# Layer norm feeding a float32 transform on one core: tokens centered beside the root, high parts rounded with the reciprocal

## The chip, the cores and the metric

The kernel runs on one core of one Trainium2 chip. The metric is the device time of one execution in microseconds (us), the median of several runs. TensorE (PE in the profile) multiplies, VectorE (DVE), ScalarE (ACT) and GpSimd (POOL) prepare its operands, SyncE (SP) and GpSimd issue the transfers.

## The reference

`x` has 2048 tokens of 640 values. It is normalised, then transformed by DFT matrices along both axes (the real part is kept) and, beside that, passed through a gated MLP; both results are added to `x`.

```python
xn = _layernorm(x, axis=-1)                       # (x - mean) / sqrt(var + 1e-5)

# FNet part
a = einsum("bsd,ed->bse", xn, dft_hid_re)
b = einsum("bsd,ed->bse", xn, dft_hid_im)
y = einsum("ts,bse->bte", dft_seq_re, a) - einsum("ts,bse->bte", dft_seq_im, b)

# gated part, D = 640, F = 1728
gate = einsum("bsd,df->bsf", xn, W_gate)
up   = einsum("bsd,df->bsf", xn, W_up)
gate = gate * (gate > 0)
z = einsum("bsf,fd->bsd", gate * up, W_down)

return x + y + z
```

All of it is float32.

## The kernel before

Every float32 operand of a product is split in two: a high part, the value rounded by ScalarE to the type that TensorE takes (`F32R`), and a low part, the value minus the high part, by VectorE or GpSimd. A product is then three: high times high, high times low, low times high (`mm3`, L127, and for the first streams `first_products`, L492, and `next_products`, L464). TensorE therefore always waits for two other engines, and the kernel orders their work by hand: `pin` (L237) keeps instructions in program order on an engine, and the lists of work in `drive` (L701) say what is loaded, prepared and multiplied when.

The work has three stages: the DFT along the tokens, gate and up projections, and the last projections. The change is in the first 71 us of the first stage, where the tokens are normalised while the transform already runs. Tokens come in eight groups g = 0 to 7 of 256 tokens: 128 partitions with `SG` = 2 tokens j each. Columns `K14` are the first 384 of the 640, `K2` the other 256. For groups 0 to 3 only `K14` is split in high and low here and `K2` is kept as float32 by a copy (`keep_a21`, L233, a transfer on the GpSimd queue); groups 4 to 7 split all 640 columns.

Each group is multiplied by two blocks of the DFT matrix, c = 0 and c = 1 (1024 columns of 128 rows, 512 KB); a group is 36 products of 512 columns, 18 for each block. In the order of TensorE:

- group 0 (`first_products`, L500 in the profile): for token j = 0 and then j = 1, high parts of the tokens times the high half block c = 0, their low parts, the same for c = 1, then the low half blocks
- groups 1 to 7, c = 0 (`next_products`, L471): 18 products, first with the high parts of token 0 (times high and low block), then of token 1, last the low parts of both
- groups 1 to 7, c = 1 (`product`, L130 to L132)

The steps of a normalisation:

- `ln_stats` (L201): two bn_stats and a bn_aggr a token on VectorE: mean and variance
- `ln_root` (L207): on ScalarE the root of variance + eps, variance + eps itself (`ve`) and the negated mean; on VectorE the reciprocal `r0` of the root and one refinement step in three small instructions, which gives the corrected multiplier `r`
- then, in `next_group` (L245), `nmr` = -mean times r on VectorE; the high part by one ScalarE activation with scale r and bias nmr; on VectorE the normalised tokens (L265) and the low part, normalised minus high (L267)
- last on VectorE the low part of block c = 1 (L125)

The low part of the next group's block c = 0 is GpSimd's (L252, two instructions for the two tokens). A tiny GpSimd instruction ahead of it (`behind_vector`, L240) reads what VectorE writes last before, so that GpSimd starts only then. In `first_group` (L279) the two tokens are handled one after the other, the first with centered tokens (`ln_center`, `ln_scale`), the second in the way of `next_group`; the low half blocks are GpSimd's but for c = 1, j = 0, which is VectorE's (L311, L285 in the profile).

The first loads are issued by SyncE in this order (`first_stream.load`, L531): tokens j = 0, half block c = 0 of j = 0, tokens j = 1, half block c = 1 of j = 0, and the two half blocks of j = 1.

The products of groups 0 to 3 and 4 to 7 add up in the same PSUM banks. After group 3 ScalarE copies the sums so far out (`finish`, L579); the products of group 4 into a bank wait for its copy.

Of the kernel before, what the change touches and what calls it, by code (L numbers as in the profile page):

```python
# [12 lines left out]
P = 128  # L13
# [45 lines left out]
def fnet_reglu_kernel(  # L59
# [147 lines left out]
    def ln_root(g, mv, js, between=()):  # L207

        mean, v, ve, sd, r0, t = (mv[:, js, i] for i in range(6))
        nm, r = (stat[:, i, g, js] for i in range(2))  # L210
        yield nc.scalar.activation(sd, v, AF.Sqrt, bias=eps_t)
        yield nc.scalar.activation(ve, v, AF.Identity, bias=eps_t)  # L212
        yield nc.scalar.activation(nm, mean, AF.Copy, scale=-1.0)
        yield nc.vector.reciprocal(r0, sd)
        yield from between
        yield nc.vector.scalar_tensor_tensor(t, r0, -0.5, ve, op0=OP.mult, op1=OP.mult)
        yield nc.vector.tensor_tensor(t, t, r0, op=OP.mult)
        yield nc.vector.scalar_tensor_tensor(r, t, 1.5, r0, op0=OP.add, op1=OP.mult)

    def ln_center(g, xs, mv, j, cs, engine):  # L220
        xc = xs[:, j, cs]
        if engine is nc.vector:
            yield nc.vector.tensor_scalar(xc, xc, mv[:, j, 0:1], None, op0=OP.subtract)
        else:
            yield nc.scalar.activation(xc, xc, AF.Identity, bias=stat[:, 0, g, j : j + 1])

    def ln_scale(g, xs, j, cs):
        xc, r = xs[:, j, cs], stat[:, 1, g, j : j + 1]
        h, l = (tokens(g)[:, j * XS + o : j * XS + o + D][:, cs] for o in (0, D))
        yield nc.scalar.activation(h, xc, AF.Copy, scale=r)  # L230
        yield nc.vector.scalar_tensor_tensor(l, xc, r, h.bitcast(F32), op0=OP.mult, op1=OP.subtract)
# [13 lines left out]
    def next_group(g, b, raw, before):  # L245

        xs, bs, mv = ln_tiles(g)
        js = slice(0, SG)
        cs = K14 if g < NH else slice(0, D)
        nm, r = (stat[:, i, g, js] for i in range(2))  # L250
        nmr = mv[:, js, 6]
# [8 lines left out]
        pin([nc.vector.tensor_tensor(nmr, nm, r, op=OP.mult)])  # L260
        pin(nc.scalar.activation(xn_block(g, cs, 0)[:, j], xs[:, j, cs], AF.Identity,  # L261
                                 bias=mv[:, j, 6:7], scale=stat[:, 1, g, j : j + 1]) for j in range(SG))
        if before is None:
            low(nc.vector, slice(0, W2))
        pin(nc.vector.tensor_scalar(xs[:, j], xs[:, j], mv[:, j, 0:1], stat[:, 1, g, j : j + 1],  # L265
                                    op0=OP.subtract, op1=OP.mult) for j in range(SG))
        late["ln"] = pin([nc.vector.tensor_tensor(xn_block(g, cs, 1), xs[:, :, cs], xn_block(g, cs, 0).bitcast(F32),  # L267
                                                  op=OP.subtract)])[0].ins
        if g < NH:
            keep_a21(g)  # L270
        if g == NG - 1:
            nc.sync.dma_start(rows.rearrange("m (g p j) -> p m g j", p=P, j=SG), stat)
        if g == 2:
            st = stage()[:, :CH].rearrange("p (j d) -> p j d", j=SG)
            for j in range(SG):
                pin([nc.scalar.activation(st[:, j], ln_place(0)[:, j, K2], AF.Copy, scale=stat[:, 1, 0, j : j + 1])])
            keep_a21(0, st)

    def first_group(b):  # L279


        xs, bs, mv = ln_tiles(0)
        part = lambda c, j: b[c][1][:, j * CH : (j + 1) * CH]
        high = lambda c, j: pin([nc.scalar.activation(b[c][0][:, 0, j], part(c, j), AF.Copy)])
        low = lambda c, j, engine: pin([engine.tensor_tensor(b[c][0][:, 1, j], part(c, j), b[c][0][:, 0, j].bitcast(F32),  # L285
                                                             op=OP.subtract)])
        d0, d14, rest = slice(0, P), slice(P, 3 * P), slice(P, D)
        places = lambda j: [tokens(0)[:, j * XS + o : j * XS + o + D] for o in (0, D)]
# [5 lines left out]
        h0, h14 = ln_scale(0, xs, 0, d0), ln_scale(0, xs, 0, d14)  # L294
        pin([next(h0)])
        pin(ln_center(0, xs, mv, 0, rest, nc.vector))
        pin([next(h14)])
# [6 lines left out]
        nm, r, nmr = stat[:, 0, 0, j1], stat[:, 1, 0, j1], mv[:, 1, 6:7]  # L304
        h, l = places(1)
        pin(ln_stats(0, xs, bs, mv, j1))
        pin(ln_root(0, mv, j1))
        high(0, 1)
        pin([nc.vector.tensor_tensor(nmr, nm, r, op=OP.mult)])
        pin(nc.scalar.activation(h[:, cs], xs[:, 1, cs], AF.Identity, bias=nmr, scale=r) for cs in (d0, d14))  # L310
# [8 lines left out]
        pin(ln_center(0, xs, mv, 1, K2, nc.scalar))  # L319
# [203 lines left out]
    def first_stream(c, name, g):  # L523
# [7 lines left out]
        def load():  # L531
            if n == 0 and c == 0:
# [15 lines left out]
        def prepare():  # L548
# [4 lines left out]
            if (n > 0 or c > 1) and "b" not in t:  # L553
                t["b"] = b = parts()
                with ExitStack() as order:
                    if c == 1:
                        order.enter_context(tc.issue_after(late["ln"]))
                    i = split(flat(b, 0), flat(b, 1), t["s"])
# [7 lines left out]
        def run():  # L566
# [3 lines left out]
            if n > 0 and c == 0:  # L570
                next_products(n, t["b"])
                return
# [5 lines left out]

        def finish():  # L579
            if g == NH - 1:  # L580
                s = (sums_a, sums_b)[c % 2]()
                for i, key in enumerate((("e1", 0), ("e1", 1), "v1")):
                    copy(s[:, i], E[c, key])
# [702 lines left out]
```

## Time and profile before

| | us |
|---|---|
| median of 3 runs | 1033.83 (1033.81 to 1034.27) |
| the profiled execution | 1033.63 |
| its span, first to last instruction | 1031.9 |
| TensorE busy | 1024.6 (99%) |
| VectorE busy | 801.1 (78%) |
| ScalarE busy | 430.1 (42%) |
| GpSimd busy | 117.3 (11%) |

The granted TensorE clock was 1.000 over the run. Rows of the timeline begin with the start in us from the start of the span and the duration in us; then come engine, line of the kernel, operation, output and input by the program's names, and how many instructions were merged (x18). What stands in brackets is the idle time before and what ended it. In rows by form the three numbers are the shortest, median and longest instruction in ns.

### The profile page before, as it was taken

How to read it: one execution, taken by the hardware profiler on the slowest of the kernel's cores; microseconds unless marked ns; L12 is line 12 of the kernel's file. 1: busy time of each engine (PE TensorE's matmuls, PEld its weight loads, DVE VectorE, ACT ScalarE, POOL GpSimd, SP SyncE). 2: the span in 40 equal slices, each digit the busy share in tenths (PEclk: the TensorE clock that was granted, in tenths of full speed). 3: DMA queues.
4: the chain of work that ended last, by engine and by line, in shares of the span. 5: the costliest groups of instructions: out<-in, count | busy, mean ns of one | idle time of the engine just before them, and what ended most of it. 6: DMA issues, size and time to landing. Idle time of an engine off the chain costs nothing.

```text
span 1031.9 us, 12494 instructions
## 1 busy us (share of the span) xinstructions
PE 1024.6 (99%) x4528; PEld 844.7 (82%) x4528; DVE 801.1 (78%) x1074; ACT 430.1 (42%) x544; POOL 117.3 (11%) x184
## 2 busy tenths in 40 slices
PE   9999999999999999999999999999999999999998
PEld 7878888888888888888888888888778888888886
DVE  7777887998989576788878988886497667886764
ACT  6654453343443333433335443443365423552521
POOL 3431001012110002321110001000000000000000
PEclk9999999999999999999999999999999999999999
DMA  8878734867968885763364665662798637986543
GB/s 307 304 266 301 261 132 167 328 234 242 372 236 314 319 308 169 253 217 133 145 246 148 221 234 215 228 256 102 240 341 294 195 126 227 377 304 214 159 154 122
DMA packets 101469, 242.73 MB, mean 235 GB/s; under 512 B 11552, under 2 KB 50976, under 8 KB 98848
## 3 DMA queue, kind: packets, MB, share of 16 engines
q1 hardware_dynamic: 83664, 171.68, 48.6%
q0 software_dynamic: 17744, 70.26, 18.3%
q8 instruction: 35, 0.57, 0.2%
q14 instruction: 26, 0.21, 0.1%
HBM read 182.12 MB, written 58.74 MB: 233 GB/s over the span
## 4 chain that ended last, share of the span: by engine, by line
PE 96%; DVE 2%; DMA 1%; ACT 1%; issue 0%; SPq 0%; DVEq 0%; ACTq 0%
PE ps L132 31%; PE ps L131 31%; PE ps L130 31%; PE ps L471 3%; PE ps L1183 1%; DMA rw<-hd 1%; DVE bs L204 0%; DMA r<-in_x 0%; ACT xs_late L261 0%; ACT xs_early L261 0%; ACT mv L212 0%; DVE mv L205 0%; DVE r L265 0%; DVE cb L125 0%; SPq L1190 0%
## 5 line engine op out<-in xcount | busy, mean ns | idle before, releaser
L130 PE MATMUL ps<-cb,wt 128*128 128x512 f32 x390 | 151.9, 390 | 0.6 <-ACT wt L124 0.6
L132 PE MATMUL ps<-cb,wt 128*128 128x512 f32 x390 | 151.9, 390 | 0.4 <-DVE wt L125 0.4
L131 PE MATMUL ps<-cb,wt 128*128 128x512 f32 x390 | 151.8, 389 | 0.0
L125 DVE TENSOR_TENSOR cb<-rw,cb 128x1024 fp32r<-128x1024 f32 x83 | 93.9, 1132 | 70.8 <-ACT cb L124 70.1
L124 ACT ACTIVATE cb<-rw 128x1024 fp32r<-128x1024 f32 x83 | 82.0, 988 | 151.7 <-PE ps L132 127.3
L124 ACT ACTIVATE cb<-raw 128x1024 fp32r<-128x1024 f32 x71 | 75.3, 1061 | 123.0 <-PE ps L132 106.3
L125 DVE TENSOR_TENSOR cb<-raw,cb 128x1024 fp32r<-128x1024 f32 x71 | 86.7, 1222 | 35.7 <-ACT cb L124 35.5
L130 PE MATMUL ps<-xs_early,gw 128*128 128x512 f32 x260 | 101.2, 389 | 0.0
L131 PE MATMUL ps<-xs_early,gw 128*128 128x512 f32 x260 | 101.2, 389 | 0.0
L132 PE MATMUL ps<-xs_early,gw 128*128 128x512 f32 x260 | 101.1, 389 | 0.0
L130 PE MATMUL ps<-cb,xs_late 128*128 128x512 f32 x232 | 90.2, 389 | 0.0
L131 PE MATMUL ps<-cb,xs_late 128*128 128x512 f32 x232 | 90.2, 389 | 0.0
L132 PE MATMUL ps<-cb,xs_late 128*128 128x512 f32 x232 | 90.2, 389 | 0.0
L121 ACT ACTIVATE gw<-z 128x1024 fp32r<-128x1024 f32 (+1 forms) x52 | 57.6, 1109 | 76.4 <-DVE z L793 76.4
L130 PE MATMUL ps<-cb,xs_early 128*128 128x512 f32 x226 | 87.9, 389 | 0.0
L131 PE MATMUL ps<-cb,xs_early 128*128 128x512 f32 x226 | 87.9, 389 | 0.0
L132 PE MATMUL ps<-cb,xs_early 128*128 128x512 f32 x226 | 87.9, 389 | 0.0
L130 PEld LDWEIGHTS ps<-cb,wt 128*128 128x128 f32 x390 | 73.2, 188 | 16.2 <-ACT wt L124 1.0
L132 PEld LDWEIGHTS ps<-cb,wt 128*128 128x128 f32 x390 | 73.2, 188 | 15.8 <-DVE wt L125 0.7
L131 PEld LDWEIGHTS ps<-cb,wt 128*128 128x128 f32 x390 | 73.2, 188 | 15.6 <-DVE cb L125 0.3
L121 ACT ACTIVATE u<-ps 128x512 f32<-128x512 f32 x52 | 31.1, 597 | 94.4 <-PE ps L132 94.4
L803 DVE TENSOR_TENSOR gw<-z,gw 128x1024 fp32r<-128x1024 f32 (+1 forms) x52 | 64.6, 1282 | 3.8 <-ACT gw L121 3.8
(197 smaller groups left out, 1981.0 us busy)
## 6 DMA issues: line engine op xcount, KB each, us to landing
raw<-in_dft SPq DMA_DIRECT2D x94, 512.0 KB, 5.5
wt<-wparts SPq DMA_DIRECT2D x66, 256.0 KB, 3.2
z<-in_wgu SPq DMA_DIRECT2D x26, 640.0 KB, 3.9
hd<-ob POOLq DMA_DIRECT2D x26, 512.0 KB, 3.7
rw<-hd SPq DMA_DIRECT2D x24, 512.0 KB, 6.6
wparts<-pw POOLq DMA_DIRECT2D x11, 1024.0 KB, 4.1
tk<-in_dft SPq DMA_DIRECT2D x16, 512.0 KB, 6.7
set<-r POOLq DMA_DIRECT2D x16, 512.0 KB, 3.3
```

The lines of the kernel that those rows point to most:

```text
L121: return nc.scalar.activation(o, i, AF.Copy)
L124: nc.scalar.activation(hi, src, AF.Copy)
L125: return nc.vector.tensor_tensor(lo, src, hi.bitcast(F32), op=OP.subtract)
L130: nc.tensor.matmul(ps, wh, mh, start=first, stop=False, skip_group_check=more)
L131: nc.tensor.matmul(ps, wh, ml, start=False, stop=False, skip_group_check=more)
L132: nc.tensor.matmul(ps, wl, mh, start=False, stop=last, skip_group_check=more)
L471: start["pe"] = pin([nc.tensor.matmul(E[0, key], xn_part(n * SG + j, d)[v == 1], b[:, int(v == 2), j], start=False, stop=n % NH == NH - 1 ...
L803: tt(self.w[:, 1, cs], self.z[:, cs], self.w[:, 0, cs].bitcast(F32), op=OP.subtract)
L1183: nc.tensor.matmul(B[key], wr[:, v, es], hr[:, cs], start=False, stop=v == 1, skip_group_check=not new)
```

## The change

- After the root, VectorE centers the tokens in place (`ln_center`, now on VectorE always), in `next_group` one token ahead of the reciprocal and one behind it.
- The high part is the centered token times the reciprocal `r0` (`ln_high`), without the refinement. The low part is centered token times the corrected `r`, minus the high part, in one scalar_tensor_tensor a token (`ln_low`). `nmr` is gone.
- `ve` is computed on VectorE, within `ln_refine`; the negated mean is an activation of its own (`ln_mean`).
- For groups 1 to 3 the columns `K2` are normalised by an instruction of their own for each token.
- In `first_group` both tokens go the same way; the low half block c = 1, j = 0 stands ahead of the second token's statistics on VectorE. In group 1 the low part of block c = 0 is two instructions.
- SyncE issues the half block c = 1, j = 0 ahead of the tokens j = 1.
- The copies of the sums of block c = 0 after group 3 are pinned on ScalarE, right behind group 4's high parts (`keep_first`).

```diff
-    def ln_root(g, mv, js, between=()):
+    def ln_first(g, mv, js):
         mean, v, ve, sd, r0, t = (mv[:, js, i] for i in range(6))
-        nm, r = (stat[:, i, g, js] for i in range(2))
-        yield nc.scalar.activation(sd, v, AF.Sqrt, bias=eps_t)
-        yield nc.scalar.activation(ve, v, AF.Identity, bias=eps_t)
-        yield nc.scalar.activation(nm, mean, AF.Copy, scale=-1.0)
-        yield nc.vector.reciprocal(r0, sd)
-        yield from between
+        return nc.scalar.activation(sd, v, AF.Sqrt, bias=eps_t), lambda: nc.vector.reciprocal(r0, sd)
+
+    def ln_mean(g, mv, js):
+        return nc.scalar.activation(stat[:, 0, g, js], mv[:, js, 0], AF.Copy, scale=-1.0)
+
+    def ln_refine(g, mv, js):
+        mean, v, ve, sd, r0, t = (mv[:, js, i] for i in range(6))
+        yield nc.vector.tensor_scalar(ve, v, EPS, None, op0=OP.add)
         yield nc.vector.scalar_tensor_tensor(t, r0, -0.5, ve, op0=OP.mult, op1=OP.mult)
         yield nc.vector.tensor_tensor(t, t, r0, op=OP.mult)
-        yield nc.vector.scalar_tensor_tensor(r, t, 1.5, r0, op0=OP.add, op1=OP.mult)
+        yield nc.vector.scalar_tensor_tensor(stat[:, 1, g, js], t, 1.5, r0, op0=OP.add, op1=OP.mult)
...
+    def ln_center(xs, mv, j, cs):
         xc = xs[:, j, cs]
...
+        return nc.vector.tensor_scalar(xc, xc, mv[:, j, 0:1], None, op0=OP.subtract)
...
+    def ln_high(g, xs, mv, j, cs):
+        return nc.scalar.activation(ln_parts(g, j, cs)[0], xs[:, j, cs], AF.Copy, scale=mv[:, j, 4:5])
+
+    def ln_low(g, xs, j, cs):
+        h, l = ln_parts(g, j, cs)
+        return nc.vector.scalar_tensor_tensor(l, xs[:, j, cs], stat[:, 1, g, j : j + 1], h.bitcast(F32),
+                                              op0=OP.mult, op1=OP.subtract)
...
     def next_group(g, b, raw, before):
...
-        pin(ln_root(g, mv, js))
-        pin([nc.vector.tensor_tensor(nmr, nm, r, op=OP.mult)])
-        pin(nc.scalar.activation(xn_block(g, cs, 0)[:, j], xs[:, j, cs], AF.Identity,
-                                 bias=mv[:, j, 6:7], scale=stat[:, 1, g, j : j + 1]) for j in range(SG))
+        root, inverse = ln_first(g, mv, js)
+        pin([root])
+        pin([ln_mean(g, mv, js)])
+        pin([ln_center(xs, mv, 0, cs)])
+        pin([inverse()])
+        pin([ln_high(g, xs, mv, 0, cs)])
+        pin([ln_center(xs, mv, 1, cs)])
+        late["high"] = pin([ln_high(g, xs, mv, 1, cs)])[0].ins
         if before is None:
-            low(nc.vector, slice(0, W2))
-        pin(nc.vector.tensor_scalar(xs[:, j], xs[:, j], mv[:, j, 0:1], stat[:, 1, g, j : j + 1],
-                                    op0=OP.subtract, op1=OP.mult) for j in range(SG))
-        late["ln"] = pin([nc.vector.tensor_tensor(xn_block(g, cs, 1), xs[:, :, cs], xn_block(g, cs, 0).bitcast(F32),
-                                                  op=OP.subtract)])[0].ins
+            for j in range(SG):
+                low(nc.vector, slice(j * CH, (j + 1) * CH))
+        pin(ln_refine(g, mv, js))
+        late["ln"] = pin(ln_low(g, xs, j, cs) for j in range(SG))[-1].ins
         if g < NH:
+            late["ln"] = pin(nc.vector.tensor_scalar(xs[:, j, K2], xs[:, j, K2], mv[:, j, 0:1], stat[:, 1, g, j : j + 1],
+                                                     op0=OP.subtract, op1=OP.mult) for j in range(SG))[-1].ins
             keep_a21(g)
...
     def first_group(b):
...
         pin(ln_stats(0, xs, bs, mv, j0))
-        pin(ln_center(0, xs, mv, 0, d0, nc.vector))
-        pin(ln_root(0, mv, j0))
+        root, inverse = ln_first(0, mv, j0)
+        pin([root])
+        pin([ln_center(xs, mv, 0, d0)])
+        pin([inverse()])
         high(0, 0)
...
+        pin([ln_high(0, xs, mv, 0, d0)])
+        pin([ln_center(xs, mv, 0, d14)])
+        pin([ln_high(0, xs, mv, 0, d14)])
+        pin(ln_refine(0, mv, j0))
         high(1, 0)
-        pin(h0)
-        pin(h14)
-        behind_vector(places(0)[1][:, 3 * P - 1 : 3 * P])
+        pin(ln_low(0, xs, 0, cs) for cs in (d0, d14))
+        behind_vector(last(0))
         low(0, 0, nc.gpsimd)
...
+        low(1, 0, nc.vector)
         pin(ln_stats(0, xs, bs, mv, j1))
-        pin(ln_root(0, mv, j1))
         high(0, 1)
...
-        low(1, 0, nc.vector)
-        whole = stage()[:, : 3 * P]
-        pin([nc.vector.tensor_scalar(whole, xs[:, 1, K14], mv[:, 1, 0:1], r, op0=OP.subtract, op1=OP.mult)])
+        root, inverse = ln_first(0, mv, j1)
+        pin([root])
+        pin([ln_center(xs, mv, 1, K14)])
+        pin([inverse()])
+        pin([ln_high(0, xs, mv, 1, K14)])
+        pin(ln_refine(0, mv, j1))
         high(1, 1)
-        pin([nc.vector.tensor_tensor(l[:, K14], whole, h[:, K14].bitcast(F32), op=OP.subtract)])
-        behind_vector(l[:, 3 * P - 1 : 3 * P])
+        pin([ln_low(0, xs, 1, K14)])
+        behind_vector(last(1))
         low(0, 1, nc.gpsimd)
         low(1, 1, nc.gpsimd)
...
                 ln_load(0, slice(0, 1))
                 get(0, 0)
+                get(1, 0)
                 ln_load(0, slice(1, 2))
-                for i in ((1, 0), (0, 1), (1, 1)):
-                    get(*i)
+                get(0, 1)
+                get(1, 1)
...
             if n > 0 and c == 0:
                 next_products(n, t["b"])
+                if n == NH - 1:
+                    keep_first()
                 return
...
+        def keep_first():
+            t["first"] = sums_a()
+            for i, key in enumerate((("e1", 0), ("e1", 1), "v1")):
+                pin([copy(t["first"][:, i], E[c, key])])
```

More of the change, by code (lines that the diff above doesn't have):

```diff
@@ L275, in next_group @@
             for j in range(SG):
-                pin([nc.scalar.activation(st[:, j], ln_place(0)[:, j, K2], AF.Copy, scale=stat[:, 1, 0, j : j + 1])])
+                late["high"] = pin([nc.scalar.activation(st[:, j], ln_place(0)[:, j, K2], AF.Copy, scale=stat[:, 1, 0, j : j + 1])])[0].ins
             keep_a21(0, st)
@@ L317, in first_group @@
+        behind_vector(last(1))
         low(0, 1, nc.gpsimd)
         low(1, 1, nc.gpsimd)
-        pin(ln_center(0, xs, mv, 1, K2, nc.scalar))
+        pin([ln_mean(0, mv, slice(0, SG))])
+        for j in range(SG):
+            pin([nc.scalar.activation(xs[:, j, K2], xs[:, j, K2], AF.Identity, bias=stat[:, 0, 0, j : j + 1])])
     def token_sets(q, step, place=None, unit=None):
@@ L557, in prepare @@
                         order.enter_context(tc.issue_after(late["ln"]))
+                        order.enter_context(tc.issue_after(late["high"]))
                     i = split(flat(b, 0), flat(b, 1), t["s"])
```

34 lines of the change are left out of this document (9 added, 25 removed).

## The prediction

> **What bounds the kernel now.** I read the page's totals and chain first, then TensorE's products in order of time over the first 71 us, then the other engines in the same stretch.
>
> ```profile
> PE 1024.6 (99%) x4528; PEld 844.7 (82%) x4528; DVE 801.1 (78%) x1074; ACT 430.1 (42%) x544; POOL 117.3 (11%) x184
> ...
> PE 96%; DVE 2%; DMA 1%; ACT 1%; issue 0%; SPq 0%; DVEq 0%; ACTq 0%
> ```
>
> TensorE is the bound: 96% of the chain that ended last is products. The change alters no product, so it can only remove or add time in which products wait. Where they wait near the layer norm is seen in their start times (second number: busy time):
>
> ```profile
> 1.03 4.79 PE L112 MATMUL ps<-warm 128*128 128x128 bf16 x48 [1.03 <-DVE warm L108]
> 6.43 9.17 PE L500 MATMUL ps<-cb,xs_early 128*128 128x512 f32 x36 [0.61 <-ACT xs_early L230]
> 15.87 4.37 PE L471 MATMUL ps<-cb,xs_early 128*128 128x512 f32 x18 [0.26 <-ACT xs_early L261]
> ...
> 24.16 4.24 PE L471 MATMUL ps<-cb,xs_early 128*128 128x512 f32 x18
> ...
> 32.32 4.24 PE L471 MATMUL ps<-cb,xs_early 128*128 128x512 f32 x18
> ...
> 40.48 4.88 PE L471 MATMUL ps<-cb,xs_late 128*128 128x512 f32 x18
> ...
> 49.28 4.29 PE L471 MATMUL ps<-cb,xs_late 128*128 128x512 f32 x18
> ...
> 57.54 4.65 PE L471 MATMUL ps<-cb,xs_late 128*128 128x512 f32 x18
> ...
> 66.13 4.64 PE L471 MATMUL ps<-cb,xs_late 128*128 128x512 f32 x18
> ...
> 70.61 0.39 PE L130 MATMUL ps<-cb,xs_late 128*128 128x512 f32 x1
> ```
>
> One product alone lasts 0.39, eighteen without a gap 4.24, so products are (4.24-0.39)/17 = 0.2265 us apart. A group is 36 products, 8.16 us. From 6.43 the first 36 ought to end at 14.59, but group 1 starts at 15.87: 1.28 lost. The intervals after that are 8.29, 8.16, 8.16, 8.80, 8.26, 8.59 and, for the last eighteen, 4.48 instead of 4.08: lost 0.13, 0, 0, 0.64, 0.10, 0.43 and 0.40. Of the 6.43 before the first product the warm-up products fill all but 0.61 of the time since 1.03. All that this change can touch is therefore about 0.6 + 1.28 + 1.70 = 3.6 us, or 0.35% of the run.
>
> **Step 1, the first product.** Before, it waits for the root, four small steps and then the rounding of the high part:
>
> ```profile
> 4.79 0.29 ACT L211 ACTIVATE mv<-mv,eps_t 128x1 f32<-128x1 f32 x1 [2.55 <-DVE mv L205]
> 4.79 0.29 DVE L223 TENSOR_SCALAR r<-r,mv 128x128 f32<-128x128 f32 x1
> ...
> 5.11 0.16 DVE L214 RECIPROCAL mv<-mv 128x1 f32<-128x1 f32 x1
> ...
> 5.26 0.61 ACT L284 ACTIVATE cb<-raw 128x512 fp32r<-128x512 f32 x1
> ...
> 5.79 0.16 DVE L218 SCALAR_TENSOR_TENSOR stat<-mv 128x1 f32<-128x1 f32 x1
> ...
> 5.98 0.91 ACT L230 ACTIVATE xs_early<-r,stat 128x128 fp32r<-128x128 f32 x2
> ...
> 6.42 0.35 DVE L231 SCALAR_TENSOR_TENSOR xs_early<-r,stat,xs_early 128x128 fp32r<-128x128 f32 x1
> ...
> 6.92 0.49 DVE L231 SCALAR_TENSOR_TENSOR xs_early<-r,stat,xs_early 128x256 fp32r<-128x256 f32 x1 [0.15 <-ACT xs_early L230]
> ...
> 7.32 0.88 DVE L204 BATCH_NORM_STATS2 bs<-r 128x6 f32<-128x320 f32 x2
> ...
> 7.64 1.28 POOL L285 TENSOR_TENSOR cb<-raw,cb 128x512 fp32r<-128x512 f32 x1
> ...
> 7.67 0.63 ACT L284 ACTIVATE cb<-raw 128x512 fp32r<-128x512 f32 x1 [0.78 <-DMA raw<-in_dft]
> ...
> 8.48 0.29 ACT L211 ACTIVATE mv<-mv,eps_t 128x1 f32<-128x1 f32 x1 [0.19 <-DVE mv L205]
> ...
> 9.81 0.69 DVE L285 TENSOR_TENSOR cb<-raw,cb 128x512 fp32r<-128x512 f32 x1
> ```
>
> The multiplier that the high part needs is now the reciprocal, ready at 5.11+0.16 = 5.27 instead of 5.79+0.16 = 5.95. Three small activations fill 4.79 to 5.26; two of them go, so the DFT block's rounding starts near 4.97 and the high part 0.53 behind it, 5.5. The first product follows 0.45 after that (6.43-5.98): 5.95, just behind the end of the warm-up, 1.03+4.79 = 5.82. Gain 0.48.
>
> **Step 2, the low part moved ahead of the second token's statistics.** VectorE now does the refinement (four small steps, 0.75), both low parts (0.35+0.49), and then the low part of the second DFT block, which stood at 9.81; only behind it come the second token's statistics. Low parts end near 7.05, and GpSimd's low part follows, as before 0.23 after them (6.92+0.49 = 7.41 to 7.64): 7.28 to 8.56. The second DFT block's first half is issued one place earlier:
>
> ```profile
> 1.65 0.42 SPq L199 DMA_DIRECT2D r<-in_x  x1
> 2.12 1.38 SPq L534 DMA_DIRECT2D raw<-in_dft  x3
> ```
> ```profile
> r<-in_x SPq DMA_DIRECT2D x1, 320.0 KB, 5.3
> ```
> ```profile
> raw<-in_dft SPq DMA_DIRECT2D x1, 256.0 KB, 5.5
> ```
>
> Token rows landed at 1.65+5.3 = 6.95, the half block at 2.12+5.5 = 7.62, so 256 KB pass in 0.67. In second place the half block ends 64 KB ahead of where the rows ended, 0.17: 6.78. Its rounding (0.63) then ends at 7.45, and VectorE could start at 7.49, when GpSimd has been subtracting for 0.2 us. Does that matter? The rows on it:
>
> ```profile
> 11.47 0.88 DVE L204 BATCH_NORM_STATS2 bs<-r 128x6 f32<-128x320 f32 x2
> 11.84 2.55 POOL L285 TENSOR_TENSOR cb<-raw,cb 128x512 fp32r<-128x512 f32 x2
> ...
> 13.38 0.21 DVE L205 BATCH_NORM_AGGREGATE mv<-bs 128x2 f32<-128x12 f32 x1
> ...
> 14.23 0.19 DVE L216 SCALAR_TENSOR_TENSOR mv<-mv 128x2 f32<-128x2 f32 x1
> ...
> 15.11 1.31 ACT L261 ACTIVATE xs_early<-r,mv,stat 128x384 fp32r<-128x384 f32 x2 [0.91 <-DVE mv L260]
> ```
> ```profile
> L216 DVE SCALAR_TENSOR_TENSOR mv<-mv x9: 159/164/191, 5.4 to 64.3; 128x2 f32<-128x2 f32 x7, 128x1 f32<-128x1 f32 x2
> ...
> L218 DVE SCALAR_TENSOR_TENSOR stat<-mv x9: 159/161/164, 5.8 to 64.7; 128x2 f32<-128x2 f32 x7, 128x1 f32<-128x1 f32 x2
> ```
>
> L216 reads two tensors. Started at 14.23 under a GpSimd subtract that ends at 11.84+2.55 = 14.39, it ends at 14.42, 0.03 behind it, and takes 0.19; its twin L218, always clear of GpSimd, never exceeds 0.164. I read this as: VectorE waits out the GpSimd operation. It is a small sign, and no row shows a long operation in that place. The bounds are no wait (VectorE 7.49 to 8.18) and a wait of 8.56-7.49 = 1.07. I take the wait. The Trainium skill ("SBUF — State Buffer", Who interferes with whom) says the same more broadly: a VectorE instruction with two SBUF inputs, or in a two-port mode such as fp32 tensor_scalar, and a GpSimd instruction that reads SBUF block each other for a whole instruction, the earlier one winning. L216's row agrees for two inputs; no row here shows it for tensor_scalar. By that page this change loses most of its gain, and without it the sum is rival 2's.
>
> With the wait, the low part ends at 8.56+0.6 = 9.15 (its 0.69 less what is set up ahead), the statistics reach the root 8.48-7.32 = 1.16 after 9.05: 10.2; reciprocal ready 10.7, high part (0.72, L261's first half) 11.45. The second token's products start near 11.5 and group 1 could start 18 products later: 15.7.
>
> **Step 3, group 1.** Low part of token two ends near 12.1; GpSimd's two follow: 12.3 to 14.85. VectorE's statistics take 13.38+0.21-11.47 = 2.12, to 14.15. Next comes the centering, new in this place: one tensor_scalar of 384 columns, 0.42 between L223's 0.29 for 128 and L313's larger form. Hidden beside the root it costs nothing; held until 14.85 it ends at 15.1. Reciprocal 15.3, high part 16.0, first product 16.05: 0.18 later than 15.87, although everything began 0.48 earlier. That eats step 1. VectorE's tail (second centering, two half lows 0.69 each, refinement 0.75, two low parts of about 0.62 each and two K2 pieces of about 0.35, both estimates between the rows for 128, 256 and 512 columns, and the block's low part, about 1.2) ends near 20.3, when product 20 asks for it at 20.4: no loss, but no reserve. If the centering is not held, it starts 0.7 earlier.
>
> **Step 4, group 4.** Before, two of the three sums copies stood behind the high parts:
>
> ```profile
> 38.70 1.72 ACT L261 ACTIVATE xs_late<-r,mv,stat 128x640 fp32r<-128x640 f32 x2
> ...
> 40.33 1.06 ACT L121 ACTIVATE sa<-ps 128x512 f32<-128x512 f32 x2
> ```
>
> They end at 41.4, when products wanted them from 40.7: the 0.64. Now all three copies stand right behind the high parts. These end about 5.0 after the previous group's last low part (0.25+2.55 GpSimd, 0.25 centering, 0.2 reciprocal, 1.72), near 39.7, and the third copy 1.6 later, 41.3, against a demand near 41.1. I leave 0.3 of the 0.64.
>
> **Step 5, groups 5 to 7.** Their 0.10+0.43+0.40 come from VectorE's long round, which idled for the root and for the high part. The new round is 2.8 (until GpSimd is done) + 0.25 + 0.16 + 0.55 + 0.75 + two low parts of 0.9 (estimate, from 0.35 at 128 and 0.49 at 256) + 1.2 = 7.5 < 8.16, so nothing is late: gain 0.93. What is added to VectorE (two centerings, refinement's first step) is covered by those same idle times; without them it would be 0.3 to 0.6 us a group. Reordered stores and loads on the GpSimd and SyncE queues serve steps far behind; with a product stream that waits for none of them they cost nothing.
>
> **Sum.** Group 1 starts at 16.05, then 0.1 for a restart, six groups 48.98, eighteen products 4.08 and 0.3: 69.5 where 70.61 stood, say 1.0 us earlier with 0.1 for what I have left out. The profiled execution took 1033.63 (span 1031.9), 0.20 under the median of the runs. Forecast 1032.6.
>
> **Rivals.** 1: VectorE wins the race of step 2. That needs the half block by 6.45, so that its rounding ends before 7.15. Then GpSimd waits instead; group 1 starts near 14.9, and the gain is 2.0: 1031.6. For: it is issued 0.47 earlier. Against: FIFO order gives 6.78. 2: nothing is held, the L216 reading being chance: group 1 near 14.7, no loss at groups 4 to 7: 2.7 saved, 1030.9; if only centering runs freely, 1.9: 1031.7. 3, slower: the second token's rows, now third in the queue, land late. Forecast is 7.62 against a use at 9.05; from there each us late is a us lost, and from 10.05 the kernel is slower. If they landed with the next group's rows, near 10.4, it would be 1034.0; to lose over 0.2% they must be later than 12.1. Against: 256 KB took 0.67. 4: the stream waits elsewhere and nothing comes of it: 1033.6.
>
> **Numbers.** Forecast 0.54, rival 1 0.17, rival 2 0.18 (both free 0.12), rival 3 0.06, rival 4 0.05. A difference under 0.2% (2.07 us) can hardly be told from none. Faster than that: 0.10 of both free, 0.08 of rival 1, 0.02 of free centering, 0.03 of the forecast: 0.23. Slower: 0.04. The range runs from both free with a little more, 1030.8, to no gain against the median, 1033.8.
>
> **What would show it.** Right: first product near 5.95; the second DFT low part on VectorE lasting over 1 us and ending behind GpSimd's; centerings of groups 1 to 7 ending just behind GpSimd's pair; group 1 near 16; intervals of 8.2 from group 4 on. Wrong: a centering of 0.42 under a running GpSimd subtract, or group 1 before 15.

## The result, and the profile after

| | before | changed |
|---|---|---|
| first comparison, median of 8 runs each | 1033.65 (1032.35 to 1034.27) | 1030.52 (1030.12 to 1034.06) |
| ratio | | 0.9979, 95% interval 0.9970 to 0.9987 |
| second comparison, median of 19 and 11 runs | 1032.89 (1031.99 to 1034.03) | 1031.25 (1030.30 to 1032.39) |
| ratio | | 0.9983, 95% interval 0.9974 to 0.9991 |
| the profiled execution | 1033.63 | 1030.23 |
| its span | 1031.9 | 1028.3 |

By the two ratios the change makes the kernel 1.8 to 2.2 us faster (0.17% to 0.21% of 1033); the medians differ by 3.1 in the first comparison and 1.6 in the second. The ratios are not the quotients of these medians, which are 0.9970 and 0.9984. The forecast was a gain of 1.0 in the profiled execution, 1.2 between the medians.

The page of the changed kernel, busy times and the chain that ended last:

```profile
PE 1022.1 (99%) x4528; PEld 844.5 (82%) x4528; DVE 805.9 (78%) x1089; ACT 427.6 (42%) x534; POOL 118.1 (11%) x184
...
PE 98%; DMA 1%; DVE 0%; SPq 0%; ACT 0%; issue 0%; DVEq 0%
```

The products are the same, and their share of the chain rose from 96% to 98%. Where they waited less is seen in the same view as before, the timeline of TensorE over the first stage (start, duration, line):

```profile
6.00 8.78 PE L510 MATMUL ps<-cb,xs_early 128*128 128x512 f32 x36 [0.56 <-ACT xs_early L231]
14.61 4.26 PE L481 MATMUL ps<-cb,xs_early 128*128 128x512 f32 x18
...
19.06 0.50 PE L131 MATMUL ps<-cb,xs_early 128*128 128x512 f32 x1
...
23.05 4.24 PE L481 MATMUL ps<-cb,xs_early 128*128 128x512 f32 x18
...
31.21 4.24 PE L481 MATMUL ps<-cb,xs_early 128*128 128x512 f32 x18
...
39.37 4.52 PE L481 MATMUL ps<-cb,xs_late 128*128 128x512 f32 x18
...
47.81 4.24 PE L481 MATMUL ps<-cb,xs_late 128*128 128x512 f32 x18
...
64.13 4.24 PE L481 MATMUL ps<-cb,xs_late 128*128 128x512 f32 x18
```

Group 6, left out here, starts at 55.97. The first product is 0.43 earlier. Group 1 starts 8.61 after it (9.44 before), and the intervals after that are 8.44, 8.16, 8.16, 8.44, 8.16, 8.16. Against 8.16, the time of 36 products, the lost time is 0.45 in group 0, 0.28 in group 1 (at the product of 19.06, which waits for the low part of block c = 1) and 0.28 in group 4. Group 7's first eighteen products now follow without a gap and end where 68.21 stands for the next product, 2.40 earlier than 70.61. So 2.4 us come from the stage that was changed.

The spans differ by 3.6, not by 2.4. The other 1.2 us lie 680 us later, where the last stage begins. The wait there, first in the kernel before, then in the changed one:

```profile
748.28 0.50 PE L130 MATMUL ps<-cb,wt 128*128 128x512 f32 x1 [0.62 <-ACT wt L124]
749.67 0.50 PE L132 MATMUL ps<-cb,wt 128*128 128x512 f32 x1 [0.37 <-DVE wt L125]
```
```profile
746.08 0.50 PE L132 MATMUL ps<-cb,wt 128*128 128x512 f32 x1 [0.35 <-DVE wt L125]
```

These products wait for ScalarE and VectorE, which split weights (`wt`) and loaded hidden values (`rw`); the loads were issued some 8 to 10 us earlier. The chain of that stretch goes through one transfer, which took 8.6 us from issue to landing before and 7.6 after:

```profile
rw<-hd SPq DMA_DIRECT2D x1, 512.0 KB, 8.6
```
```profile
rw<-hd SPq DMA_DIRECT2D x1, 512.0 KB, 7.6
```

The change does not touch this transfer. How far its length varies from one execution to the next is looked at below.

Now the race that the prediction was about. The timeline of ScalarE, VectorE and GpSimd in the changed kernel:

```profile
6.25 0.62 ACT L292 ACTIVATE cb<-raw 128x512 fp32r<-128x512 f32 x1
...
7.02 0.68 DVE L293 TENSOR_TENSOR cb<-raw,cb 128x512 fp32r<-128x512 f32 x1
7.19 0.57 POOL L248 TENSOR_TENSOR root_t<-xs_early 128x1 f32<-128x1 f32 x1 [6.74 <-DVE xs_early L235]
...
7.61 0.64 ACT L292 ACTIVATE cb<-raw 128x512 fp32r<-128x512 f32 x1 [0.74 <-DMA raw<-in_dft]
7.71 1.28 POOL L293 TENSOR_TENSOR cb<-raw,cb 128x512 fp32r<-128x512 f32 x1
...
10.94 2.54 POOL L293 TENSOR_TENSOR cb<-raw,cb 128x512 fp32r<-128x512 f32 x2
...
12.60 1.10 DVE L225 TENSOR_SCALAR r<-r,mv 128x384 f32<-128x384 f32 x1
...
13.70 0.39 DVE L225 TENSOR_SCALAR r<-r,mv 128x384 f32<-128x384 f32 x1
```

ScalarE rounds the half block c = 1 from 6.25 on, so it had landed by then; VectorE subtracts from 7.02 to 7.70. GpSimd's one-column operation, which takes 0.19 elsewhere, takes 0.57 and ends at 7.76: GpSimd waited for VectorE and not the other way round. At 12.60 the roles are reversed. The centering of 384 columns, 0.39 in the row below it, lasts 1.10 and ends at 13.70, 0.22 behind GpSimd's pair (10.94 + 2.54 = 13.48).

### The profile page after: what moved, and what is told of

It is laid out like the page before. It is cut to its first block, busy times and chain, and to the rows that moved or that the text cites. A ratio compares the mean times of both kernels' runs of the same rounds, so it can differ in the third digit from the quotient of the medians.

```text
span 1028.3 us, 12486 instructions
## 1 busy us (share of the span) xinstructions
PE 1022.1 (99%) x4528; PEld 844.5 (82%) x4528; DVE 805.9 (78%) x1089; ACT 427.6 (42%) x534; POOL 118.1 (11%) x184
## 4 chain that ended last, share of the span: by engine, by line
PE 98%; DMA 1%; DVE 0%; SPq 0%; ACT 0%; issue 0%; DVEq 0%
PE ps L132 31%; PE ps L131 31%; PE ps L130 31%; PE ps L481 3%; PE ps L1204 1%; PE ps L510 1%; DMA rw<-hd 1%; DMA r<-in_x 0%; SPq L1211 0%; DVE wt L125 0%; DVE bs L204 0%; DVE y L1214 0%; ACT cb L292 0%; SPq L1100 0%; SPq L1071 0%
```

## The experiments

Each kernel ran with the kernel before on the same chip. Each row is one profiled execution; the time beside it is one run of the kernel before, in the last two rows the median of 19. All numbers but the times come from the timeline of TensorE: the start of the first product and of groups 1, 4 and 7, and the span from group 7's start to the end ("rest"). The same number for the kernel before holds 0.40 that group 7 itself lost.

| kernel | first | group 1 | group 4 | group 7 | rest | time | before beside it |
|---|---|---|---|---|---|---|---|
| before | 6.43 | 15.87 | 40.48 | 66.13 | 965.8 | 1033.63 | |
| changed | 6.00 | 14.61 | 39.37 | 64.13 | 964.2 | 1030.23 | 1033.63 |
| loads in the old order | 6.13 | 16.07 | 41.01 | 65.82 | 964.0 | 1031.64 | 1032.73 |
| low half in the old place | 6.16 | 14.88 | 39.77 | 64.57 | 964.8 | 1031.25 | 1032.73 |
| both old | 6.09 | 15.29 | 40.01 | 64.78 | 964.4 | 1031.01 | 1032.73 |
| sums copies not pinned | 6.03 | 14.65 | 39.45 | 65.17 | 964.0 | 1030.96 | 1032.73 |
| corrected root | 6.65 | 16.25 | 41.43 | 66.55 | 964.2 | 1032.60 | 1034.52 |
| GpSimd longer | 6.18 | 14.81 | 41.91 | 67.06 | 964.1 | 1033.04 | 1034.52 |
| two waits | 6.15 | 14.78 | 40.56 | 65.04 | 964.2 | 1031.17 | 1034.52 |
| loads of x later | 6.11 | 15.15 | 40.03 | 64.83 | 963.5 | 1030.13 | 1034.52 |
| three waits | 6.07 | 14.76 | 39.41 | 63.89 | 963.5 | 1029.27 | 1032.76 |
| uncentered high | 6.10 | 14.94 | 39.66 | 64.76 | 963.9 | 1030.53 | 1032.76 |
| changed, again | 6.15 | 14.97 | 39.86 | 64.69 | 964.9 | 1031.37 | 1032.89 |
| three waits, again | 6.09 | 14.72 | 39.25 | 63.73 | 963.5 | 1029.27 | 1032.89 |

By its time alone a single execution can't be compared, since the rest of the same code varies by 1 us (963.9 to 964.9 over ten executions). The first stage varies too. Eight executions of the table have the changed kernel's code up to group 1's first product (changed, sums copies not pinned, GpSimd longer, two waits, loads of x later, three waits, and the two repeats). In them group 1 starts between 8.61 and 9.04 after the first product. Where the first stage is wholly the changed kernel's, group 7 starts at 64.13, 64.69 and 64.83 (changed, changed again, loads of x later). A difference at group 1 under 0.4, or at group 7 under 0.7, is therefore not told from this spread by one execution; a loss within one group can be, where it repeats better (group 4 lost 0.28, 0.35 and 0.32 in those three).

**Loads in the old order.** Only the two lines in `first_stream.load` go back:

```diff
                 get(0, 0)
+                ln_load(0, slice(1, 2))
                 get(1, 0)
-                ln_load(0, slice(1, 2))
                 get(0, 1)
```

> The changed kernel with the first loads in the old order (second token's rows ahead of the half block c = 1). Theory H (an instruction of VectorE that reads two tensors, or a tensor_scalar, and a GpSimd subtract do not run together, the earlier holds the other): the half block lands near 7.6, its rounding ends near 8.25, GpSimd's subtract has run since about 7.2 to 8.5, so VectorE's low half ends about 0.55 behind it, near 9.05; group 1 starts at 15.6 to 15.9 instead of 14.61 and the second part of group 7 at 69.2 to 69.5 instead of 68.21. Theory F (they run side by side; only the chain's length counts): the low half takes 0.69 whatever GpSimd does, the centering of group 1 takes 0.4 under GpSimd's subtract, group 1 starts near 15.4 and group 7's second part near 68.8.

This kernel has what the prediction assumed of the changed one: the half block comes too late for VectorE to be first. Its timeline:

```profile
7.47 1.27 POOL L293 TENSOR_TENSOR cb<-raw,cb 128x512 fp32r<-128x512 f32 x1
8.29 1.00 DVE L293 TENSOR_TENSOR cb<-raw,cb 128x512 fp32r<-128x512 f32 x1 [1.06 <-ACT cb L292]
...
10.37 0.42 DVE L225 TENSOR_SCALAR r<-r,mv 128x384 f32<-128x384 f32 x1
...
11.57 4.52 PE L510 MATMUL ps<-cb,xs_early 128*128 128x512 f32 x18 [0.22 <-ACT xs_early L231]
...
16.07 0.73 PE L481 MATMUL ps<-cb,xs_early 128*128 128x512 f32 x2
```

VectorE's low half lasts 1.00 instead of 0.69 and ends at 9.29, 0.55 behind GpSimd's 8.74. The prediction had 9.15 for that end, 11.5 for the second token's products (here 11.57) and 16.05 for group 1 (here 16.07). The centering at 10.37, with no GpSimd operation beside it, takes 0.42. So the prediction's working of steps 2 and 3 holds, but for a kernel whose half block is late. Of the two theories in the expectation, H fits: the low half is held behind GpSimd. The starts came a little later than H had them (16.07 for 15.6 to 15.9, and 69.90 for 69.2 to 69.5 at group 7's second part).

**Low half in the old place.** VectorE's low half stands behind the second token's high part again, with the new order of loads:

```diff
-        low(1, 0, nc.vector)
         pin(ln_stats(0, xs, bs, mv, j1))
...
         pin([ln_high(0, xs, mv, 1, K14)])
+        low(1, 0, nc.vector)
         pin(ln_refine(0, mv, j1))
```

> The changed kernel with VectorE's low half of the second block put back behind the second token's high part; the new load order stays. H: GpSimd's first subtract runs from about 7.25 to 8.5 unhindered, the second token's centering is held behind it (0.6 instead of 0.44), its high part still comes near 9.5, in time; group 1 at 14.4 to 14.7, group 7's second part at 68.0 to 68.3: the step moved ahead was not needed. F: the same starts, but a centering of 0.44. If the step ahead is what brought the gain, group 1 comes at 15.2 or later.

Group 1 starts 8.72 after the first product, within the 8.61 to 9.04 of the changed kernel's code: with the new order of loads, no gain from moving the low half ahead is seen. (At 14.88 group 1 came later than the 14.4 to 14.7 expected.) VectorE's and GpSimd's timeline show what happens instead:

```profile
7.50 1.29 POOL L293 TENSOR_TENSOR cb<-raw,cb 128x512 fp32r<-128x512 f32 x1
...
8.34 0.67 DVE L225 TENSOR_SCALAR r<-r,mv 128x384 f32<-128x384 f32 x1
```

Without the low half in front, the statistics are done earlier, but then the centering meets GpSimd's subtract: it ends at 9.01, 0.22 behind GpSimd's 8.79.

**Both old.** Both edits together.

> Both old: load order and place of VectorE's low half of the second block. H and F: the second block's products wait for its rounding, near 8.3 as before the change, 0.6 to 0.7 lost there; group 1 at 15.1 to 15.4, group 7's second part at 68.7 to 69.0. This is what the early load of the second block is worth.

Group 1 comes 9.20 after the first product. From there, the new order of loads alone brings it to 8.72, the new place alone worsens it to 9.94, and both together give 8.61 to 9.04. So the place costs 0.74 with the old order, and with the new one it makes no difference beyond the spread.

**Sums copies not pinned.** The call of `keep_first` is left out, so the copies go to `finish` as in the kernel before.

> The changed kernel without the pinned copies of the sums after group 3 (the scheduler places them as before the change). If the pinning is what shortened group 4's wait from 0.64 to 0.28, the wait returns to 0.5 to 0.8 and group 7's second part comes at 68.5 to 68.8; if the earlier high parts did it, 0.2 to 0.4 and 68.1 to 68.4. Groups 1 to 3 are unchanged (14.61, 23.05, 31.21).

The timeline of TensorE and ScalarE around group 4:

```profile
39.45 0.39 PE L481 MATMUL ps<-cb,xs_late 128*128 128x512 f32 x1
39.88 1.07 ACT L121 ACTIVATE sa<-ps 128x512 f32<-128x512 f32 x2
...
40.52 4.42 PE L481 MATMUL ps<-cb,xs_late 128*128 128x512 f32 x17 [0.68 <-ACT sa L121]
...
48.85 0.39 PE L481 MATMUL ps<-cb,xs_late 128*128 128x512 f32 x1
```

Two of the copies fall behind the block's rounding again. Group 4 lasts 48.85 - 39.45 = 9.40 and loses 1.24 (0.5 to 0.8 were expected), where the changed kernel loses 0.28. The pinning is worth 0.96 here, more than the 0.64 that group 4 lost before; group 4 now asks for the copies about 1 us earlier.

**Corrected root.** The refinement stands ahead of the high part again, which takes the corrected multiplier; all else is the changed kernel.

```diff
-        return nc.scalar.activation(ln_parts(g, j, cs)[0], xs[:, j, cs], AF.Copy, scale=mv[:, j, 4:5])
+        return nc.scalar.activation(ln_parts(g, j, cs)[0], xs[:, j, cs], AF.Copy, scale=stat[:, 1, g, j : j + 1])
...
         pin([inverse()])
+        pin(ln_refine(g, mv, js))
         pin([ln_high(g, xs, mv, 0, cs)])
...
-        pin(ln_refine(g, mv, js))
```

> The changed kernel, but the high part is scaled with the corrected root: the refinement (four small VectorE steps) stands ahead of the high part everywhere. H and F alike: the first product is 0.5 to 0.8 later (6.5 to 6.8), group 1 at 15.1 to 15.5, and since groups 3 to 7 have slack only the start and groups 1 and 2 pay: group 7's second part at 68.7 to 69.2. If the uncorrected root is worth nothing, all starts stay within 0.1.

```profile
6.65 8.97 PE L510 MATMUL ps<-cb,xs_early 128*128 128x512 f32 x36 [0.86 <-ACT xs_early L231]
16.25 0.73 PE L481 MATMUL ps<-cb,xs_early 128*128 128x512 f32 x2 [0.63 <-ACT xs_early L231]
```

In this view of TensorE the first product is 0.65 later than in the changed kernel and group 1 1.64. By group 7 it is 2.42 later, 66.55 against 64.13, and with the 4.08 of eighteen products its second part starts at 70.63, where the kernel before had 70.61. Without the rounding by the reciprocal the rest of the change gives nothing in this stage that this execution shows. That is more than expected (16.25 for 15.1 to 15.5 at group 1, 70.63 for 68.7 to 69.2): groups 3 and 4, where the expectation saw slack, lost 0.54 and 0.64. The parts are not a sum, though: undoing the order of loads alone costs 1.69 at group 7, undoing the pinned copies 1.04 (1.13 and 0.48 against the repeated run of the changed kernel). One edit has no run of its own: the rounding of the block c = 1 is now issued only behind the group's high parts.

**GpSimd longer.** In groups 2 to 7 GpSimd's first subtract is done twice, which changes no value.

> The changed kernel with GpSimd's first subtract of groups 2 to 7 done twice (the same values written again), so GpSimd works 3.8 instead of 2.54 beside VectorE's statistics. H: the first centering of groups 2 to 7 ends 0.2 to 0.35 behind GpSimd's last subtract again, so it lasts 2.3 to 2.6 instead of 1.06 to 1.3; VectorE's round becomes longer than the 8.16 of a group, group 2 starts near 24.0 and group 7's second part at 70.0 to 71.2. F: the centerings keep their lengths and group 7's second part stays at 68.1 to 68.4.

The timeline of GpSimd and VectorE in group 2:

```profile
19.45 4.04 POOL L255 TENSOR_TENSOR cb<-raw,cb 128x512 fp32r<-128x512 f32 x3
...
21.15 1.18 DVE L225 TENSOR_SCALAR r<-r,mv 128x384 f32<-128x384 f32 x1
22.33 1.37 DVE L225 TENSOR_SCALAR r<-r,mv 128x384 f32<-128x384 f32 x1
```

The expectation had the first centering wait for all three subtracts, 2.3 to 2.6 us; it does not. Seen one by one, the second subtract runs from 20.82 to 22.12; the centering is held until then, ends 0.21 behind it and goes in between. The third subtract takes 1.41 instead of 1.29 and holds the second centering, which ends at 23.70, 0.21 behind GpSimd's 23.49. So the hold lasts one instruction, and here the earlier one goes first. The delay piles up: VectorE's statistics of groups 2, 3 and 4 start at 19.12, 27.35 and 35.54 (18.93, 26.25 and 33.41 in the changed kernel), and the copies of the sums, behind group 4's second high part, are 2 us late for their banks: group 4 at 41.91, 2.54 later than in the changed kernel.

**Two waits.** The K2 pieces of group 1 go behind the low part of its block c = 1 (for the 0.28 in group 1), and the three sums copies between the two high parts of group 4 (for the 0.28 there).

> The changed kernel with two edits against its two remaining waits: in group 1 the two pieces of columns K2 stand behind the block's low part instead of ahead of it, and the sums copies stand between the two high parts of group 4 instead of behind both. If the 0.28 in group 1 is the low part coming 0.65 late and the 0.28 in group 4 the copies standing behind the second high part, both go: intervals of 8.16 to 8.2 throughout and group 7's second part at 67.6 to 67.8. If group 2's statistics, now behind K2, become late instead, group 2 loses 0.2 to 0.5 and nothing is won.

The second half did what it should: group 4 lasts 48.72 - 40.56 = 8.16. The first half failed; group 2 came 9.31 after group 1 instead of 8.44, and group 7's second part at 69.12 where 67.6 to 67.8 were expected:

```profile
18.44 0.73 DVE L279 TENSOR_SCALAR r<-r,mv,stat 128x256 f32<-128x256 f32 x2
...
19.49 0.88 POOL L240 DMA_DIRECT2D xs_early<-r  x1 [5.86 <-DVE r L279]
20.40 0.20 POOL L248 TENSOR_TENSOR root_t<-cb 128x1 f32<-128x1 f32 x1
20.55 2.54 POOL L255 TENSOR_TENSOR cb<-raw,cb 128x512 fp32r<-128x512 f32 x2
21.11 2.20 DVE L225 TENSOR_SCALAR r<-r,mv 128x384 f32<-128x384 f32 x1
...
24.09 1.20 PE L493 MATMUL ps<-cb,xs_early 128*128 128x512 f32 x4 [0.98 <-ACT xs_early L231]
```

The transfer of the K2 pieces is issued by GpSimd and stands ahead of its pair. With the pieces later, the issue is later, the pair starts at 20.55 instead of 19.25, and the centering is held for 2.20 us.

**Loads of x later.** In the last stage, the three loads of x for the first of its outputs are issued at step 5 instead of step 3, behind the hidden values and weights that are needed first.

> The changed kernel with the loads of the three output tiles y at the start of the last stage issued two places later, behind the last rows of the hidden values. If the wait of the products near 746 (1.0 in all in the profiled run of the changed kernel, about 2.0 in that of the kernel before) comes from the place in SyncE's queue behind the y loads, it goes, and the span is 0.8 to 1.2 shorter than 1028.3 at the same 68.21; if the transfer takes 7 to 9 us for lack of bandwidth, the wait stays within 0.5 of what it was.

No product waits any more at the start of the last stage, and the rest is 963.5 instead of 964.2, 0.7 less (0.8 to 1.2 were expected). Group 1 started late in this run, 9.04 behind the first product. A load landed late: ScalarE, in its timeline, waited 1.93 us for the half block c = 0 of j = 1, where it waited 0.74 in the changed kernel, and the root of the second token stands behind that rounding.

```profile
8.91 0.63 ACT L292 ACTIVATE cb<-raw 128x512 fp32r<-128x512 f32 x1 [1.93 <-DMA raw<-in_dft]
```

**Three waits.** The sums copies between the high parts and the later loads of x are kept; the K2 pieces of group 1 go behind group 2's second centering instead.

> The changed kernel with three of its remaining waits addressed: the K2 pieces of group 1 stand behind group 2's second centering on VectorE (not behind the block's low part, which had put their transfer ahead of GpSimd's pair), the three sums copies stand between the two high parts of group 4, and one transfer of the last stage is read back two steps later. Theory (GpSimd's pair starts when VectorE's last low part ends, and the centering ends 0.22 behind the pair): the block's low part of group 1 ends 0.7 earlier, near 18.3, GpSimd's pair of group 2 starts near 18.5 and not 19.25, and the intervals after group 1 are 8.16, 8.16, 8.16, 8.16, 8.16: 0.28 and 0.28 us gone; with the 0.7 us of the last stage the time is near 1029.0. Rival (VectorE's round of group 2, 0.7 us longer, is the next bound): group 3 or 4 late by 0.3 to 0.7, time near 1029.5.

```profile
17.43 1.22 DVE L125 TENSOR_TENSOR cb<-raw,cb 128x1024 fp32r<-128x1024 f32 x1
18.87 2.54 POOL L255 TENSOR_TENSOR cb<-raw,cb 128x512 fp32r<-128x512 f32 x2
21.93 0.73 DVE L281 TENSOR_SCALAR r<-r,mv,stat 128x256 f32<-128x256 f32 x2
```

The block's low part ends at 18.65 (19.01 in the changed kernel), GpSimd's pair starts at 18.87 and the K2 pieces stand behind it. The intervals from group 1 on are 8.33 and then five times 8.16; the rival's late group 3 did not come. The pair was expected near 18.5, and 0.17 is still lost in group 1. (The expectation calls the loads of x one transfer; they are three.)

**Uncentered high.** In groups 1 to 3 the high part is made from raw tokens, so that it does not wait for the centering.

```diff
-        pin([ln_high(g, xs, mv, 0, cs)])
...
+            for j in range(SG):
+                pin([nc.scalar.activation(mv[:, j, 6:7], stat[:, 0, g, j : j + 1], AF.Copy, scale=mv[:, j, 4:5])])
+                late["high"] = pin([nc.scalar.activation(ln_parts(g, j, cs)[0], xs[:, j, cs], AF.Identity,
+                                                         bias=mv[:, j, 6:7], scale=mv[:, j, 4:5])])[0].ins
```

> The changed kernel, but in groups 1 to 3 the high part doesn't wait for the centering: ScalarE makes it from the raw tokens with scale r0 and bias -mean times r0 (two small activations more), and VectorE centers into a buffer of its own, for the low part alone. VectorE's and GpSimd's work stays. If it is the centering held by GpSimd that sets the start of group 1, group 1's high part starts about 0.35 earlier and its first product at 14.25 (with a first product near 6.0). If VectorE's chain up to the block's low part sets what follows, the 0.35 is given back there: the wait for that low part in group 1 grows from 0.28 to about 0.6, group 2 starts at the same place as in the changed kernel, near 23.1, and the time is the same, 1030.2. Rival: the gain stays, 1029.9 and all later groups 0.35 earlier.

Inconclusive for group 1. ScalarE, in its timeline, waited 0.66 us for the next block to land before it could round it, and the root stands behind that rounding:

```profile
12.30 1.06 ACT L257 ACTIVATE cb<-raw 128x1024 fp32r<-128x1024 f32 x1 [0.66 <-DMA raw<-in_dft]
```

The root came at 13.27 and the high part at 14.18; the centering would have been held for only some 0.4 us from there, until GpSimd's end at 13.64, and the added activations take about as much. Group 2 came 17.24 after the first product (17.05 in the changed kernel, 17.39 in its repetition), and group 4 lost 0.62: no gain to be seen, and what the hold costs group 1 by itself stays open.

**The changed kernel and the three waits, five rounds each on one chip.**

> The changed kernel again, timed against the kernel before in five rounds on one chip. If the 3.4 us of the single profiled executions are 2.4 us in the first stage and up to 1.2 us from a transfer of the last stage whose landing varies from run to run, the ratio is near 0.9975, between 0.9970 and 0.9980. If all 3.4 us belong to the change, 0.9967.

> The version with three remaining waits addressed, in five rounds on the same chip. Its one look gave 1029.27 beside 1032.76 for the kernel before. Of the 1.2 us that the three edits should take off the changed kernel 0.3 to 0.5 are in the first stage and 0.7 in the last, where the wait depends on a transfer that varies: expected 0.8 to 1.4 us under the changed kernel, ratio to the kernel before 0.9963 to 0.9969. Rival (the last stage's wait comes back elsewhere): 0.3 to 0.5 us under the changed kernel.

The changed kernel: 1031.25 against 1032.89, ratio 0.9983, interval 0.9974 to 0.9991. The point is a little above the expected 0.9975, the interval holds it, and 0.9967, all 3.4 us for the change, is excluded. The three waits: 1029.40, ratio 0.9970, interval 0.9960 to 0.9980, and 1.85 us under the changed kernel between the medians, more than the 0.8 to 1.4 expected, though the ratio is just above the expected 0.9963 to 0.9969. The profiled executions say where: group 7 starts 0.96 earlier, and the rest is 963.5 against 964.9, since the changed kernel waited twice in this execution:

```profile
746.00 0.49 PE L130 MATMUL ps<-cb,wt 128*128 128x512 f32 x1 [0.19 <-ACT wt L124]
747.39 0.50 PE L132 MATMUL ps<-cb,wt 128*128 128x512 f32 x1 [0.36 <-DVE wt L125]
```

In the three executions with the loads of x later the rest was 963.5 each time; in the ten others with the changed kernel's last stage it lay between 963.9 and 964.9. So the wait goes with the order of loads in that stage. The transfer that took 7.6 in the first execution of the changed kernel took 8.2 in the repeated one, with the same code (a row of the chain that ended last):

```profile
738.12 8.23 DMA rw<-hd
```

With it 0.7 of the 1.2 us came back. The other 0.5 stay open: the kernel before has only one traced execution, and its rest, 965.4 without group 7's own loss, lies above all ten. In the repeated run the first stage alone gives 70.61 - (64.69 + 4.08) = 1.84, near the 1.64 between the medians of that comparison.

## Why the prediction was right and where it was wrong

**What was right.** TensorE's products bound the kernel, and the change moved only their waits. Step 1: the first product at 5.95, measured 6.00. Step 4: 0.3 left in group 4, measured 0.28. Step 5: groups 5 to 7 without loss, measured intervals 8.16. The reading of L216, on which step 2 rested, held in every form: the first centerings of groups 2 and 3 end 0.23 behind GpSimd's pair in the changed kernel, those of groups 4, 6 and 7 (640 columns) 0.35. What the Trainium skill ("SBUF — State Buffer", Who interferes with whom) says of two-input instructions and of tensor_scalar in a two-port mode agrees: 1.10 instead of 0.39 for the centering, 1.00 instead of 0.69 for the subtract, and GpSimd's 0.57 instead of 0.19 where VectorE was first. It says that the loser blocks fully; here a held instruction still took up to 0.2 us less behind the release than alone, as the last section shows.

**The step that failed is the landing time in step 2.** The forecast put the half block at 6.78, so that GpSimd would win the race. It landed near 5.95. The issues of the changed kernel on SyncE's queue, and the landings of the two half blocks and of the first alone:

```profile
1.19 0.89 SPq L544 DMA_DIRECT2D raw<-in_dft  x2
```
```profile
raw<-in_dft SPq DMA_DIRECT2D x2, 256.0 KB, 3.7
```
```profile
raw<-in_dft SPq DMA_DIRECT2D x1, 256.0 KB, 3.1
```

The second was issued at about 1.65; the number of the pair is the middle of its two, so the second took about 2 x 3.7 - 3.1 = 4.3. In the repeated run of the changed kernel the same transfer has a row of its own:

```profile
raw<-in_dft SPq DMA_DIRECT2D x1, 256.0 KB, 4.6
```

That is 6.25, still ahead of the 6.45 that rival 1 asked for. The working subtracted 64 KB from the tokens' landing at 6.95, which came from one execution. The same transfer in the same place took 5.3 in that execution and 4.2 with the old order of loads in the changed kernel:

```profile
r<-in_x SPq DMA_DIRECT2D x1, 320.0 KB, 4.2
```

From 4.2 the same working gives 5.7 and the opposite winner. A landing spreads over 1 us, the winner turned on 0.33 (6.78 against 6.45), and the prediction treated the number as fixed. In all ten profiled executions with the low half and its load both moved VectorE won.

**So rival 1 happened**, which had a chance of 0.17. It gave 14.9 for group 1 and 1031.6. Measured were 14.61 and 1030.2, of which 1.2 came from the last stage, so 1031.4 like for like; the repeated run gave 14.97 and 1031.4. The rivals beside it did not come. Rival 2 had nothing held, and the centering at 12.60 was. Rival 3 had the second token's rows late; in the changed kernel they landed 4.8 us after their issue at 2.12, at 6.92, and VectorE's statistics read them from 7.62 on.

**Step 3, group 1.** "0.18 later than 15.87" did not come, as a consequence of step 2. "No loss, but no reserve" for the low part of the block was right on the side of VectorE and wrong on that of the products: VectorE's tail ended at 19.01 and not near 20.3, but group 1 asks 1.3 earlier than before, so 0.28 were lost.

**The sum and the range.** The forecast, 1032.6, stands for the kernel with the old order of loads: group 7's second part at 69.5 predicted, at 65.82 + 4.08 = 69.90 measured; most of the difference is in group 1, which lost 0.46 there where the sum put 0.1. The range began at 1030.8; the first median is 1030.52, the second 1031.25. That 1031.4 lies inside the range owes nothing to step 2: the range was wide because the rivals were priced. What the range lacked was the varying rest: no step looked beyond 71 us, and the profiled execution of the kernel before, from which the sum was made, had a rest 1.2 us longer than that of the changed kernel.

## What to carry to other kernels

A race between two engines for a shared resource has two outcomes that differ by whole instructions; if its winner follows from a landing time, take that time from several executions before choosing a winner, or, with one execution, give both outcomes a like chance. When a step is put behind another engine's long instruction, count that engine's queue too, transfers it issues included: a transfer issued 1.3 us later cost 0.9 us because GpSimd's subtracts stood behind it. A difference of about 1 us between two single executions should be split by stage before it is explained, since a stage that the change never touched can hold much of it (1.2 of 3.6 us here).

## What was not expected of the hardware

- The hold goes by single instructions, not by pairs: with three GpSimd subtracts in a row a waiting centering went in between, and the next subtract took 1.41 instead of 1.29. In group 5 of the changed kernel, two subtracts lasted 2.86 instead of 2.54 for the same reason.
- A held instruction does not need its whole time after the release: the centering of 384 columns ended 0.22 behind GpSimd where it takes 0.39 to 0.42 alone, and the subtract of 512 columns 0.55 behind where it takes 0.69. So 0.14 to 0.2 us of it are done by the time of the release.
- With loads of 256 to 320 KB issued 0.45 us apart, one and the same load landed 5.3, 4.2 and 4.8 us after its issue in three executions with the old order of loads.
